# Attention and ResMLP in one kernel: the first batch's q and k loaded ahead of v with its exponentials in one chain, and lambda multiplied in PSUM in all blocks but the last

## The chip, the cores and the metric

One core of one Trainium2 chip. The time is the device time of one execution in microseconds (us). For one core there is no second die to compare with, so a run is called slow only when it lies over 1.5% above the fastest of the same kernel. The median of before is 381.8 us.

## The reference, cut to what matters

```python
# q, k, v: (8 batches, 8 heads, 576, 64); scores against k and v averaged over 8 rows
k_p = k.reshape(B, H, 72, 8, D).mean(axis=3);  v_p = v.reshape(B, H, 72, 8, D).mean(axis=3)
attn = softmax(q @ k_p.T / 8);  x = attn @ v_p            # x as (B, 576, 512)
a1 = alpha1 * x + beta1
u = x + lam * (w_tok @ a1)                                # token mix, over the 576 rows
ch = relu((alpha2 * u + beta2) @ w_ch1) @ w_ch2           # MLP 512 -> 2048 -> 512
out = u + lam * ch
```

The kernel cuts the 8 x 576 rows into 36 chunks of 128 and works on four chunks at a time: nine MLP blocks, numbered 0 to 8. While the MLP of block n runs on TensorE, the attention and token mix of batch n+1 are woven between its matmuls; so only batch 0 has nothing to hide behind. The 64 last rows of each head ("rest") are loaded and cast apart.

## The kernel before

The parts that the change and the argument touch. A number such as `at` is a place in the block's order of issue, counted in groups of TensorE work. Names in the views: `ps_...` lies in PSUM (`ps_sc` scores, `ps_h` and `ps_ch` the two matmuls of the MLP, `ps_tok` the token mix), `ET` are the exponentials, `x_tm` the normalised heads, `xs` these times lambda and alpha1, which the token mix takes in.

```python
    # loads of batch 0, in this order on the SyncE queue
    load_qk(0, 0); load_rem(0); load_v(0, 0); load_v_rem(0); load_qk(0, 1); load_v(0, 1)
    ...
    def sum_k(b, u, eng):                 # pool k: 16 -> 8 -> 4 rows, then a sum into bf16
        t = st1[b]["raw"][u][:, 1]
        for n in (4, 2):
            eng.tensor_tensor(out=t[:, :, 0:n], in0=t[:, :, 0:n], in1=t[:, :, n:2 * n], op=ALU.add)
        eng.tensor_tensor(out=bf, in0=..., in1=..., op=ALU.add)
    ...
    def scale_w2(g, i):                   # 16 of these, in block 1
        nc.vector.tensor_tensor(out=w2[g][:, i], in0=w2[g][:, i], in1=lam_bc, op=ALU.mult)
    ...
    def mlp_B(n, m, part):                # second matmul of the MLP; ps_ch has two PSUM buffers
        for j in js:
            nc.tensor.matmul(out=ps, lhsT=Hj[n, j][:, 128 * m:128 * m + 128],
                             rhs=w2[j // 4][:, j % 4, cols], start=(j == 0), stop=(j == NJ - 1))
        if part == 3 or last and part == 1:
            if n == 0:                    # block 0 runs before w2 is scaled
                nc.vector.tensor_tensor(out=ps, in0=lam_bc, in1=ps, op=ALU.mult)
            nc.vector.tensor_tensor(out=u, in0=u, in1=ps, op=ALU.add)
            nc.sync.dma_start(out=..., in_=u)
    ...
    # batch 1 (late = True) is woven into block 0
    todo = [(2.0 if late else -2.0, lambda: cast_rem(b, nc.gpsimd)), ...]     # rest q, rest k
    for u in range(2):                    # q_at = 0.5 and 6.0 for batch 1
        todo.append((q_at, lambda u=u, copy=copy: cast_q(b, u, copy)))
        todo.append((q_at + 0.1, lambda u=u: sum_k(b, u, nc.gpsimd)))
    ...
    if n == 1:
        for j in range(NJ):
            todo.append((0.5 + 1.1 * j, lambda j=j: scale_w2(j // 4, j % 4)))
```

The softmax here doesn't subtract the row's maximum and nothing guards it: scores larger than these inputs give would overflow.

## Time and profile before

| | before |
|---|---|
| device time, median of 4 runs | 381.81 us (381.28 to 382.54) |
| span of the profiled run, TensorE busy | 379.3 us, 361.6 us |
| first token mix starts, first MLP matmul starts | 27.28, 35.96 us |
| blocks 0 to 8, from first MLP matmul to first MLP matmul | 45.63, 43.46, 39.06, 38.86, 39.06, 38.87, 39.06, 27.62, 31.72 us |

A block is the time from its first MLP matmul to that of the next block, so the nine blocks and the 35.96 us ahead of them add up to the span. A block without waits is some 39 us when a batch is woven in and 27.6 us when none is (block 7).

### The profile page before, as it was taken

Reading aid. Unit: us, or ns where it says so; the run is one execution under the profiler, and the core shown is the slowest. Engines: PE = TensorE matmul, PEld = TensorE weight load, DVE = VectorE, ACT = ScalarE, POOL = GpSimd, SP = SyncE. Lnnn points to the kernel's source line nnn. Section 1 sums busy time; section 2 is a strip of 40 time slices with the busy share of each in tenths; the row PEclk is TensorE's granted clock in tenths of the full one; section 3 lists DMA queues with packets and bytes.
Section 4 is the critical chain, followed back from the end, with each engine's and each line's share of the span. In section 5 each row is a group of like instructions: output and inputs, shape, how many; then the busy total and the mean of one; then the engine's idle time right before and its main releaser. Section 6 shows DMA issues by size and latency. Waiting matters only on the chain.

```text
span 379.3 us, 6099 instructions
## 1 busy us (share of the span) xinstructions
PE 361.6 (95%) x2346; PEld 199.4 (53%) x2346; DVE 217.5 (57%) x441; ACT 202.6 (53%) x406; POOL 99.5 (26%) x141
## 2 busy tenths in 40 slices
PE   6579999999889999999999999999999999999995
PEld 2356754455444555455545554555455545544544
DVE  6976437799996528733864378436762685011011
ACT  3643887048721695179615970598049814721710
POOL 7743939003920082008200640055000000000000
PEclk9968999999999999999999999999999999999999
DMA  7999893029201561147013801290110011002002
GB/s 251 258 212 334 218 273 123 2 83 329 74 29 57 190 214 28 57 158 244 28 57 111 293 29 29 92 337 6 53 55 3 1 57 54 3 28 83 2 28 83
DMA packets 19602, 43.27 MB, mean 114 GB/s; under 512 B 2221, under 2 KB 4593, under 8 KB 19574
## 3 DMA queue, kind: packets, MB, share of 16 engines
q1 hardware_dynamic: 17488, 37.89, 29.4%
q0 software_dynamic: 1920, 4.86, 6.9%
q8 instruction: 18, 0.29, 0.3%
q10 hardware_dynamic: 166, 0.14, 0.1%
q14 instruction: 10, 0.08, 0.1%
HBM read 38.30 MB, written 9.44 MB: 126 GB/s over the span
## 4 chain that ended last, share of the span: by engine, by line
PE 82%; DVE 13%; ACT 1%; DMA 1%; issue 1%; SPq 0%
PE ps_ch L548 30%; PE ps_h L525 29%; PE ps_tok L494 12%; DVE w L319 3%; PE ps_sc L429 3%; DVE x_tm L453 2%; PE ps_uT L509 2%; PE ps_av L446 2%; DVE xs L460 1%; PE ps_q L346 1%; DMA qk_raw<-in_k_dram 1%; DVE qk_raw L132 1%; PE ps_kp L377 1%; DVE rec L451 1%; DVE v_u L392 1%
## 5 line engine op out<-in xcount | busy, mean ns | idle before, releaser
L548 PE MATMUL ps_ch<-w,Hj 128*128 128x512 bf16 (+1 forms) x592 | 140.2, 373 | 1.1 <-DVE w L319 1.1
L525 PE MATMUL ps_h<-u_fm,w 128*128 128x512 bf16 (+1 forms) x592 | 134.6, 373 | 0.2 <-ACT u_fm L511 0.2
L530 ACT ACTIVATE Hj<-ps_h,bias_cols 128x512 bf16<-128x512 f32 x144 | 96.7, 691 | 38.0 <-PE ps_h L525 37.1
L525 PEld LDWEIGHTS <-w 128*128 128x128 bf16 x592 | 64.8, 114 | 48.4 <-issue 0.9
L548 PEld LDWEIGHTS <-Hj 128*128 128x128 bf16 x592 | 55.7, 98 | 48.6 <-issue 0.5
L511 ACT COPY u_fm<-ps_uT 128x512 bf16<-128x512 bf16 x36 | 21.1, 586 | 89.1 <-PE ps_uT L509 89.0
L431 ACT ACTIVATE ET<-ps_sc 128x288 f16<-128x288 f32 (+1 forms) x128 | 52.4, 488 | 16.1 <-PE ps_sc L429 15.9
L555 DVE TENSOR_TENSOR u_sb<-u_sb,ps_ch 128x512 f32<-128x512 f32 (+1 forms) x37 | 24.8, 669 | 56.9 <-PE ps_ch L548 56.6
L494 PE MATMUL ps_tok<-xs,wtT 128*128 128x512 bf16 (+1 forms) x200 | 50.3, 385 | 2.0 <-DVE xs L460 1.9
L384 DVE CAST kpT<-ps_kp 64x288 bf16<-64x288 f32 x29 | 13.2, 455 | 49.2 <-PE ps_kp L380 49.0
L496 DVE TENSOR_TENSOR u_sb<-x_tm,ps_tok 128x512 f32<-128x512 f32 (+1 forms) x40 | 27.5, 686 | 22.5 <-PE ps_tok L494 22.5
L115 POOL CAST rem_q<-rem_raw 128x256 bf16<-128x256 f32 x7 | 3.1, 440 | 139.6 <-DMA rem_raw<-in_q_dram 139.6
L453 DVE TENSOR_TENSOR x_tm<-ps_av,rec 128x320 f32<-128x320 f32 x64 | 31.4, 491 | 2.3
L429 PE MATMUL ps_sc<-qT,kpT 128*128 128x288 bf16 (+1 forms) x128 | 29.2, 307 | 3.5 <-DVE x_tm L453 1.1
L494 PEld LDWEIGHTS <-wtT 128*128 128x128 bf16 (+1 forms) x200 | 19.3, 98 | 25.1 <-issue 3.6
L132 POOL TENSOR_TENSOR qk_raw<-qk_raw 128x512 f32<-128x512 f32 (+1 forms) x28 | 29.6, 1058 | 1.1
L498 DVE TENSOR_TENSOR u_bf<-u_sb,al_bc 128x512 bf16<-128x512 f32 (+1 forms) x39 | 27.8, 713 | 1.4
L446 PEld LDWEIGHTS <-ET 72*128 72x128 f16 (+1 forms) x256 | 16.8, 102 | 16.4 <-ACT ET L431 2.2
L451 DVE RECIPROCAL rec<-ps_av 128x5 f32<-128x5 f32 x64 | 12.0, 188 | 20.1 <-PE ps_av L449 19.6
L460 DVE TENSOR_TENSOR xs<-x_tm,lamal_bc 128x512 bf16<-128x512 f32 x30 | 21.9, 729 | 1.0
L446 PE MATMUL ps_av<-vp,ET 72*128 72x66 f16 (+1 forms) x256 | 19.0, 199 | 0.6 <-DVE x_tm L453 0.4
L392 DVE TENSOR_TENSOR v_u<-v_u 128x512 f32<-128x512 f32 (+1 forms) x30 | 17.6, 587 | 1.1 <-DMA v_u<-in_v_dram 0.4
(110 smaller groups left out, 290.8 us busy)
## 6 DMA issues: line engine op xcount, KB each, us to landing
qk_raw<-in_q_dram SPq DMA_DIRECT2D x16, 512.0 KB, 5.5
qk_raw<-in_k_dram SPq DMA_DIRECT2D x16, 512.0 KB, 6.3
v_u<-in_v_dram SPq DMA_DIRECT2D x32, 256.0 KB, 7.0
out_dram<-u_sb SPq DMA_DIRECT2D x32, 256.0 KB, 2.3
w<-in_moe_w_ch_dram POOLq DMA_DIRECT2D x2, 1024.0 KB, 12.8
w<-in_moe_w_ch_dram POOLq DMA_DIRECT2D x4, 512.0 KB, 9.8
rem_raw<-in_q_dram SPq DMA_DIRECT2D x8, 128.0 KB, 7.8
rem_raw<-in_k_dram SPq DMA_DIRECT2D x8, 128.0 KB, 5.3
```

Of the source, the lines that this page charges most:

```text
L132: eng.tensor_tensor(out=t[:, :, 0:n], in0=t[:, :, 0:n], in1=t[:, :, n:2 * n], op=ALU.add)
L429: nc.tensor.matmul(out=ps_sc[0:n, 0:288], lhsT=kpT_pool[u][:, j, r, 72 * hh:72 * hh + n], rhs=st["qT"][u][:, h % 4, :])
L431: nc.scalar.activation(out=ET[0:n, 64 + j:64 + S + j:2], in_=ps_sc[0:n, 0:288], func=AF.Exp, bias=0.0, scale=1.0 / 64)
L446: nc.tensor.matmul(out=av[:, c, :], lhsT=ET[:, m0:m0 + 256:2], rhs=vp1)
L453: nc.vector.tensor_tensor(out=x[:, :, dd:dd + D], in0=av[:, :, 0:64], in1=rec.unsqueeze(2).to_broadcast((P, 5, D)), op=ALU.mult)
L460: eng.tensor_tensor(out=xs[:, 0:4, cols], in0=x[:, 0:4, cols], in1=lamal_bc[:, cols].unsqueeze(1).to_broadcast((P, 4, D * (h1 - h0))), op= ...
L494: nc.tensor.matmul(out=ps_tok, lhsT=wtT[0:kk, at, t0:t0 + P], rhs=xs[0:kk, sc, :], start=(sc == 0), stop=(sc == 4))
L496: nc.vector.tensor_tensor(out=s["u"][p0:p1, :], in0=st1[b]["x"][p0:p1, c, :], in1=ps_tok[p0:p1, 0:DM], op=ALU.add)
L498: eng.tensor_tensor(out=s["u_bf"][p0:p1, :], in0=s["u"][p0:p1, :], in1=al2_bc[p0:p1, :], op=ALU.mult)
L525: nc.tensor.matmul(out=ps_h[:, t0:t1], lhsT=w1_of(cc, j), rhs=u_fm[n][:, cc, t0:t1], start=(cc == 0), stop=(cc == 3))
L530: nc.scalar.activation(out=t, in_=ps_h, func=AF.Relu, bias=bias_cols[:, j:j + 1], scale=1.0)
L548: nc.tensor.matmul(out=ps, lhsT=Hj[n, j][:, 128 * m:128 * m + 128], rhs=w2[j // 4][:, j % 4, cols], start=(j == 0), stop=(j == NJ - 1))
```

## The change

Two parts that touch each other nowhere. *Lambda*: `out = u + lam * ch` was had by scaling w2 once, 16 VectorE products in block 1. Now each block but the last multiplies its accumulator in PSUM, four products a block, and a scaled copy of w2 for block 8 is made in block 7, where VectorE is nearly idle. *First batch*: load the second half of q and k ahead of v, so that the exponentials of all eight heads can run on ScalarE in one chain; take casts, copies and products off VectorE; set up w_tok before the first token mix and not between the mixes. (In the part cut below, the two dummy matmuls ahead of the first mix, `keep_warm(2)`, also go.)

```diff
@@ loads @@
     load_qk(0, 0)
     load_rem(0)
+    load_qk(0, 1)
     load_v(0, 0)
     load_v_rem(0)
-    load_qk(0, 1)
     load_v(0, 1)
@@ constants @@
-    ET_pool = consts([P, S + 128], F16, "ET", 4)
+    ET_pool = consts([P, S + 128], F16, "ET", 6)
+    nc.vector.tensor_tensor(out=vecs[0:1, 1], in0=vecs[0:1, 1], in1=vecs[0:1, 0], op=ALU.mult)
@@ lambda @@
-    def scale_w2(g, i):
-        nc.vector.tensor_tensor(out=w2[g][:, i], in0=w2[g][:, i], in1=lam_bc, op=ALU.mult)
+    w2s = {}
+    def scale_w2(j):
+        if j % 8 == 0:
+            w2s[j // 8] = work.tile([P, 8, DM], BF, tag="qk_raw", bufs=2, name="w2_scaled")
+        nc.vector.tensor_tensor(
+            out=w2s[j // 8][:, j % 8], in0=w2[j // 4][:, j % 4], in1=lam_bc, op=ALU.mult)
+    def w2_of(n, j, cols):
+        return w2s[j // 8][:, j % 8, cols] if n == NBLK - 1 else w2[j // 4][:, j % 4, cols]
@@ mlp_B @@
-                             rhs=w2[j // 4][:, j % 4, cols], start=(j == 0), stop=(j == NJ - 1))
+                             rhs=w2_of(n, j, cols), start=(j == 0), stop=(j == NJ - 1))
-            if n == 0:
+            if n < NBLK - 1:
                 nc.vector.tensor_tensor(out=ps, in0=lam_bc, in1=ps, op=ALU.mult)
@@ first batch, cut @@
-    cast_rem(0, nc.gpsimd, nc.vector.tensor_copy)
+    cast_rem(0, nc.gpsimd)
+    cast_q(0, 1, nc.gpsimd.tensor_copy)
...
-    att_V(0, 0, nc.vector.tensor_copy)
     att_S(0, 2)
-    att_Vrem(0, nc.vector.tensor_copy)
     att_S(0, 3)
-    att_F(0, 1)
-    sum_k(0, 1, nc.vector)
+    sum_v(0, 0)
+    att_Vrem(0, nc.scalar.copy)
+    att_K(0, 1, nc.scalar.copy)
+    att_V(0, 0, nc.vector.tensor_copy)
     sum_v(0, 1, nc.gpsimd)
+    att_S(0, 4)
...
+    att_X(0, 4, 6, nc.gpsimd)
     load_w2(0)
     setup_wtok(0, nc.scalar.copy)
     att_AV(0, 6)
+    load_qk(1, 0, nc.vector)          # and the other loads of batch 1
+    ...
+    setup_wtok(1, nc.scalar.copy)
+    att_AV(0, 7)
+    att_X(0, 6, 8)
+    setup_rowsum(0); setup_wtok(2, nc.scalar.copy); setup_rowsum(1); setup_wtok(3, nc.scalar.copy)
     mix_T(0, 0)
-    setup_wtok(2, nc.scalar.copy)
-    setup_wtok(3, nc.scalar.copy)
@@ blocks @@
-        if n == 1:
+        if n == NBLK - 2:
             for j in range(NJ):
-                todo.append((0.5 + 1.1 * j, lambda j=j: scale_w2(j // 4, j % 4)))
+                todo.append((0.5 + 1.5 * j, lambda j=j: scale_w2(j)))
```

More of the change, by code (lines that the diff above doesn't have):

```diff
@@ L425, in att_S @@
         u, r, hh = h // 4, h // 2 % 2, h % 2
-        ET, n = ET_pool[h % 4], P if hh else SPG
+        ET, n = ET_pool[(8 * b + h) % 6], P if hh else SPG
         for j in range(2):
@@ L567 @@
     nc.scalar.copy(out=lam_bc, in_=ps_lam)
-    ps_al1 = broadcast(1)
+    ps_lamal = broadcast(1)
+    nc.scalar.copy(out=lamal_bc, in_=ps_lamal)
     cast_q(0, 0, nc.vector.tensor_copy)
@@ L572 @@
     sum_k(0, 0, nc.vector)
-    cast_rem(0, nc.gpsimd, nc.vector.tensor_copy)
+    cast_rem(0, nc.gpsimd)
+    cast_q(0, 1, nc.gpsimd.tensor_copy)
     keep_warm(2)
-    att_Frem(0, (0, 1), nc.scalar.copy)
-    att_K(0, 0, nc.scalar.copy)
-    sum_v(0, 0)
+    att_Frem(0, (0,), nc.scalar.copy)
+    att_K(0, 0, nc.vector.tensor_copy, nc.scalar.copy)
+    att_Frem(0, (1,), nc.vector.tensor_copy)
+    row_of_xs(0, nc.vector)
+    load_wtok()
     sum_v_rem(0, nc.gpsimd)
-    nc.vector.tensor_tensor(out=lamal_bc, in0=lam_bc, in1=ps_al1, op=ALU.mult)
-    cast_q(0, 1, nc.vector.tensor_copy)
-    load_wtok()
     for g in range(2):
@@ L585 @@
     att_S(0, 1)
-    att_V(0, 0, nc.vector.tensor_copy)
-    att_S(0, 2)
-    att_Vrem(0, nc.vector.tensor_copy)
-    att_S(0, 3)
-    att_F(0, 1)
-    sum_k(0, 1, nc.vector)
+    sum_k(0, 1, nc.vector)
+    att_F(0, 1)
+    att_S(0, 2)
+    att_S(0, 3)
+    sum_v(0, 0)
+    att_Vrem(0, nc.scalar.copy)
+    att_K(0, 1, nc.scalar.copy)
+    att_V(0, 0, nc.vector.tensor_copy)
     sum_v(0, 1, nc.gpsimd)
+    att_S(0, 4)
     att_AV(0, 0)
     att_AV(0, 1)
-    att_K(0, 1, nc.scalar.copy, nc.vector.tensor_copy)
-    att_S(0, 4)
+    att_S(0, 5)
     att_AV(0, 2)
-    att_S(0, 5)
+    att_X(0, 0, 2, nc.gpsimd)
     att_AV(0, 3)
-    att_X(0, 0, 2, nc.gpsimd)
+    att_X(0, 2, 4, nc.gpsimd)
     att_S(0, 6)
@@ L603 @@
     att_S(0, 7)
-    row_of_xs(0, nc.vector)
     att_AV(0, 4)
-    att_X(0, 2, 4, nc.gpsimd)
+    att_AV(0, 5)
+    att_X(0, 4, 6, nc.gpsimd)
     load_w2(0)
-    att_AV(0, 5)
     setup_wtok(0, nc.scalar.copy)
     att_AV(0, 6)
-    att_X(0, 4, 6)
-    att_AV(0, 7)
-    setup_wtok(1, nc.scalar.copy)
-    setup_rowsum(0)
-    setup_rowsum(1)
-    att_X(0, 6, 8)
     load_qk(1, 0, nc.vector)
@@ L622 @@
     load_v(1, 1)
-    keep_warm(2)
+    setup_wtok(1, nc.scalar.copy)
+    att_AV(0, 7)
+    att_X(0, 6, 8)
+    setup_rowsum(0)
+    setup_wtok(2, nc.scalar.copy)
+    setup_rowsum(1)
+    setup_wtok(3, nc.scalar.copy)
     mix_T(0, 0)
-    setup_wtok(2, nc.scalar.copy)
-    setup_wtok(3, nc.scalar.copy)
+    setup_rowsum(2)
+    mix_T(0, 1)
+    setup_rowsum(3)
     setup_vectors()
-    mix_T(0, 1)
-    setup_rowsum(2)
-    setup_rowsum(3)
     mix_T(0, 2, nc.gpsimd)
```

## The prediction

> **What bounds the kernel now.** I read the page's busy shares first (TensorE 361.6 us of 379.3, 95%, the next engine VectorE 57%), then cut the span into stages at the matmul groups, then followed the chain of waits inside the two stages that stand out. The table of stretches, with the columns span, busy time of each engine, granted TensorE clock, DMA share:
>
> ```profile
> core 0: us, PE busy (x) PEld busy (x) DVE busy (x) ACT busy (x) POOL busy (x), PEclk, DMA share, GB/s
> 0.00:35.96 35.96, 26.70 (x181) 15.37 (x182) 27.19 (x69) 17.07 (x38) 20.01 (x41) 0.86 0.97 257
> 35.96:81.59 45.63, 44.52 (x353) 26.30 (x352) 29.28 (x56) 27.03 (x57) 23.67 (x31) 1.00 0.53 151
> 81.59:125.01 43.42, 39.98 (x256) 21.40 (x255) 39.44 (x68) 22.80 (x46) 14.33 (x14) 1.00 0.34 119
> 125.01:164.07 39.06, 39.06 (x260) 21.66 (x259) 23.32 (x48) 22.97 (x47) 10.43 (x14) 1.00 0.36 119
> 320.00:347.70 27.70, 27.70 (x130) 13.60 (x129) 2.75 (x4) 11.00 (x16) 0.00 (x0) 1.00 0.10 38
> ```
>
> Rows one to four: the first batch's attention (no MLP matmul until 35.96), MLP block 0, block 1, block 2. Blocks 2 to 6 all take 38.9 to 39.1 us with TensorE never idle. Block 1 does the same matmuls and takes 43.42, with VectorE at 39.44 of it: 4.4 us more than block 2. The last row is block 7, where VectorE has 2.75 us of work in 27.70. So TensorE bounds everything except the first 36 us and block 1, and only those two can be shortened.
>
> The chain of waits in the first stage (start, length, what):
>
> ```profile
> 11.53 0.72 DVE q_bf L124
> ...
> 13.59 0.70 DVE qk_raw L132
> ...
> 14.31 1.75 DVE qk_raw L132
> ...
> 21.63 1.35 DVE xs L259
> ...
> 26.44 0.70 DVE xs L460
> ...
> 27.28 1.83 PE ps_tok L494 x5
> 29.12 1.07 PE ps_w L274 x10
> ```
>
> From 11 us to 27 us it is nearly all VectorE: the second half of q is cast there, then k is pooled there (its middle step takes 1.75 us, while the same step of the first half took 0.43), and a one-row product (xs L259, 1.35 us) stands in the middle of it. The first token mix begins at 27.28. From there to 35.96, 8.68 us, TensorE is always busy but the granted clock is 0.80, and ten transposes of w_tok (1.07 us) lie in between. In block 1 the chain names the scaling of w2:
>
> ```profile
> 84.46 2.49 DVE w L319 x4
> ...
> 98.25 4.09 DVE w L319 x3
> ```
>
> and the two kinds of product with lambda (columns after the count: min/median/max ns):
>
> ```profile
> L319 DVE TENSOR_TENSOR w<-w,lam_bc x16: 675/684/1755, 84.5 to 105.9; 128x512 bf16<-128x512 bf16 x16
> L554 DVE TENSOR_TENSOR ps_ch<-lam_bc,ps_ch x4: 685/690/697, 77.6 to 83.1; 128x512 f32<-128x512 f32 x4
> ```
>
> **What the Trainium skill says.** "Perfetto Trace Analysis", Optimization Strategy: a kernel can have several regimes with different most-contended engines, and one looks for the gaps inside each. The table above agrees. "SBUF — State Buffer", Who interferes with whom: a VectorE instruction with two SBUF inputs contends with a GpSimd instruction that reads SBUF, one with at most one SBUF input does not. The trace agrees: w2 scaling (two SBUF inputs) ranges from 0.675 to 1.755 us while GpSimd pools k, the product in PSUM (one SBUF input) stays within 0.685 to 0.697, though GpSimd was idle then, so that half isn't tested. "TensorE: Matmul & The Clock Gate", What's actually happening: after an idle window of about 3.4 us the clock halves. Here TensorE was busy 0.55 us in 15 to 18, and the granted clock in 18 to 24 was 0.50. "DMA: Bandwidth & Descriptors", Issuing engines are not separate DMA queues: all transfers interleave on the same engines. The DMA share of 0.97 over the first stage says that moving one load forward moves another back.
>
> **Part 1, lambda.** Removed from block 1: 16 scalings of w2, 13.7 us of VectorE (sum of the groups between 84.4 and 106.6). Put into block 7: the same 16, about 0.69 each = 11 us, beside 2.75 us of old work and 4 new products of 0.69 in 27.70 us, with GpSimd idle: hidden. The scaled copy takes the buffers of raw q and k, free by then. Added in blocks 1 to 7: four products in PSUM each, 4 x 0.69 = 2.8 us per block; block 0 has them already and block 8 stays without. Block 1 falls to a normal block: 43.42 - 39.06 = 4.4 us gained, a little less for the new products. In blocks 2 to 6 VectorE has 23 of 39 us, so 2.8 fit by sum, but not everywhere. The first accumulation of a block ends in the middle of the heads' normalisation, and from there VectorE works without a gap until the last xs columns, on which the token mix waits. In block 2 those end at 152.40 and the mix begins at 152.42: no slack, and 0.69 more goes straight to TensorE, less the 0.18 that TensorE itself would still be busy. In block 3 they end at 190.89 and TensorE gets there at about 191.6: 0.7 of slack, which just holds 0.69. So I take 0.5 us for blocks 2, 4 and 6 (whose batch is odd) and 0.15 for 1, 3 and 5: 2.0 in all. The later products fall between token mixes, where VectorE has 1.8 us of gaps in 10 us. **Net of part 1: -2.4 us.**
>
> **Part 2, the first batch.** The loads: 1.05 MB of q and k move ahead of 0.66 MB of v. By the bytes moved up to each time I put the second q at about 9.0 us and k at 10.5 (estimates; before they were used at 11.5 and 13.6). The cast of that q goes to GpSimd, also the cast of the rest rows; the rest of v goes from VectorE to ScalarE (2 x 0.42), the fourth copy of pooled k too (0.46), the third xs product to GpSimd (0.97). VectorE loses 0.54 + 0.67 (lam x alpha) + 0.80 + 0.84 + 0.46 + 0.97 = 4.3 us and the contention in k's pooling (1.3 us in the middle step). It gains one row product of 0.69 ahead of the first q cast, 0.3 us of fills for two more ET buffers, a k copy of 0.46 and a q copy of about 0.25: 1.7.
>
> Start: the row product waits for alpha (4.6 us) and delays the first cast by 0.35; the second broadcast matmul (2 us) waits for the row product and holds the q transposes from 6.6 to 7.4. ScalarE then copies lamal before q. So the first scores come at about 10.7 instead of 9.99, 0.7 us lost. Then ScalarE carries the chain: 16 exponentials at about 0.37 pitch (6.0), the q copy 1.0, v's rest 0.84, two k copies 0.8: 8.6 us plus about 1 us of waits, from 11.2 to about 20.8 (before: 22.2). VectorE's normalisation of eight heads (0.67 each) follows it and ends at about 23.8, and GpSimd's three xs products at 1.27 + 0.45 each, starting near 19.7, end at about 24.9; the last one on VectorE ends near 25. The first mix can begin at about 25.1: **-2.2 us**. Behind it the four mixes run with only small work between: 8.68 less 1.07 of w_tok transposes, less about half a microsecond if the clock is higher because TensorE idled less: 7.1. **-1.6 us**. Batch 1's loads are released at about 23 instead of 27.4, so block 0 is not held by them; w1's first half landed at 23.4 and might come 1 to 2 us later, still ahead of its first use near 31. Block 0 keeps its 45.6 us.
>
> Sum: -2.4 - 2.2 - 1.6 = -6.2. 381.9 - 6.2 = 375.7; I shade it to 375.2 for a clock that may not drop at all.
>
> **Rivals.** (a) The xs products on GpSimd, or the longer start, eat the new order: GpSimd's were 1.27 us against 0.69 on VectorE, and L464 took 0.91 once under contention. Then the first mix stays near 27 and only part 1 remains: 378.5 to 379.5. (b) The extra 28 products cost a full 0.69 or more in each of six blocks, because VectorE is in order and each of four delays can reach TensorE: 4 to 6 us lost, part 1 becomes nothing or negative, total 377.5 to 380. For it: block 2's zero slack. Against: only the first product of a block lies in a saturated run. (c) The clock never halves and VectorE's lighter load carries through (VectorE alone could finish xs near 22.4, counted from k's pooling at 11.6): first mix at 23, mixes in 6.5 us, 6.5 us gained at the start, total 372 to 373. (d) The DMA engines, full until 41 us, hold block 0 when it starts earlier. Against: the loads were finished by 41 and batch 1's last are needed near 44.
>
> **Range.** The threshold of 2% lies at 374.3, less than one microsecond below the estimate; the start could give 2 to 7, lambda 0 to 4. 80% range 371.5 to 378.5. A slowdown over 2% would need both parts to fail.
>
> **What would show it.** Right: block 1 at 39 to 39.5 us; block 2 about 0.5 longer, block 3 almost unchanged; block 7 at 27.7 still; first mix near 25, first MLP matmul near 32, with GpSimd's xs or the last VectorE xs ahead of it in the chain. Wrong: blocks 2 to 6 at 40 us, a gap ahead of block 8, exponentials that end after 22, or weights waited for at 31.

## More of the kernel before

The main views are in the prediction. One more is needed for what came after: what GpSimd does with batch 1 at the start of block 0. The columns are start, length, engine, line, operation, output and inputs, shapes, count, and in brackets an idle time ahead of it with what ended it.

```profile
35.68 1.03 POOL L124 CAST q_bf<-qk_raw 128x1024 bf16<-128x1024 f32 x1
36.68 2.52 POOL L132 TENSOR_TENSOR qk_raw<-qk_raw 128x512 f32<-128x512 f32 x2
...
39.95 0.40 POOL L115 CAST rem_q<-rem_raw 128x256 bf16<-128x256 f32 x1
```

Cast of q, pooling of k, cast of the rest rows of q follow each other without a gap: no bracket stands in these lines, so batch 1's transfers had landed.

## The result, and the profile after

The changed kernel takes 376.28 us (median of 4 runs, 375.66 to 376.92) against 381.81: the ratio is 0.985, with a 95% interval of 0.983 to 0.988. Within 2%, but clearly not equal. A ratio here is the mean time of one kernel's fast runs over that of the other's of the same rounds, so not quite the ratio of the medians quoted. In other rounds the gain was smaller: an unaltered second run of the changed kernel (below) gave 0.993 [0.989, 0.997].

Ledger of the two profiled spans (379.3 and 374.2 us):

| stage | before | after | difference | predicted |
|---|---|---|---|---|
| to the first token mix | 27.28 | 25.50 | -1.78 | -2.2 |
| first mix to first MLP matmul | 8.68 | 6.55 | -2.13 | -1.6 |
| block 0 | 45.63 | 46.90 | **+1.27** | 0 |
| block 1 | 43.46 | 39.11 | -4.35 | -4.4 and a little back |
| blocks 2, 4, 6 | 39.06, 39.06, 39.06 | 39.70, 39.64, 39.51 | +1.67 | +1.5 |
| blocks 3, 5 | 38.86, 38.87 | 38.92, 38.85 | +0.04 | +0.3 |
| block 7 | 27.62 | 27.62 | 0 | 0 |
| block 8 | 31.72 | 31.90 | +0.18 | 0 |
| sum | 379.3 | 374.2 | -5.1 | -6.2 |

The table of stretches of the kernel after, columns as in the prediction's (span, busy time of TensorE, its weight loads, VectorE, ScalarE, GpSimd, granted clock, DMA share, GB/s). The rows are the first stage, blocks 0, 1 and 2, and block 7:

```profile
0.00:32.05 32.05, 23.36 (x178) 13.42 (x180) 22.75 (x68) 18.45 (x40) 22.93 (x45) 0.95 0.96 243
32.05:78.95 46.90, 44.36 (x346) 26.30 (x351) 29.22 (x56) 27.23 (x57) 23.64 (x31) 1.00 0.59 177
78.95:118.06 39.11, 38.75 (x252) 21.33 (x255) 27.09 (x55) 22.37 (x46) 10.58 (x14) 1.00 0.39 132
118.06:157.76 39.70, 38.96 (x256) 21.65 (x259) 25.90 (x52) 22.95 (x47) 10.41 (x14) 1.00 0.36 117
314.60:342.20 27.60, 27.49 (x128) 13.58 (x128) 15.16 (x24) 11.00 (x16) 0.00 (x0) 1.00 0.10 39
```

VectorE has 22.75 us of work in the first stage (27.19 before), 27.09 in block 1 (39.44 before) and 15.16 in block 7 (2.75 before), and block 7 is no longer for it. The first stage's DMA share is 0.96 as before: it moved the same bytes in less time. Block 0 has the same work on every engine as before and is longer, so it must contain a wait. The chain of waits of the kernel after, of the first 40 us (start, length, what):

```profile
6.21 7.98 DMA rem_v_raw<-in_v_dram
...
23.42 0.49 DVE x_tm L464
...
25.84 9.24 DMA rem_raw<-in_k_dram
35.08 1.26 POOL qk_raw L132
...
37.95 0.35 POOL rem_q L115
38.30 0.05 issue
38.35 0.28 PE ps_qr L372 x2
```

Two long transfers stand in it. The first, the rest rows of v, pushed back by the q and k now loaded ahead of it, sets when values and heads can begin: it landed at about 14.2, ScalarE copied its product at 16.3 and the pooled k behind that, and the exponentials of heads 4 to 7 began at 17.93. So the last exponentials end at 22.10, hardly earlier than in before (22.18):

```profile
21.26 0.84 ACT L442 ACTIVATE ET<-ps_sc 128x288 f16<-128x288 f32 x2 [0.15 <-PE ps_sc L440]
```

```profile
20.67 1.51 ACT L431 ACTIVATE ET<-ps_sc 72x288 f16<-72x288 f32 x4
```

What comes earlier is what follows: VectorE's last normalisation ends at 24.55 (before 26.41). The second transfer is a new thing: batch 1's loads, issued at 24.0 instead of 27.4, land at about 35.0, and GpSimd and then TensorE wait for them. (The chain names the rest rows of k, which ended last on that queue; GpSimd's own instruction reads the main k.) GpSimd's timeline shows it, to be held against the lines of before:

```profile
31.76 1.03 POOL L124 CAST q_bf<-qk_raw 128x1024 bf16<-128x1024 f32 x1
35.06 2.09 POOL L132 TENSOR_TENSOR qk_raw<-qk_raw 128x512 f32<-128x512 f32 x2 [2.27 <-DMA rem_raw<-in_k_dram]
...
37.89 0.40 POOL L115 CAST rem_q<-rem_raw 128x256 bf16<-128x256 f32 x1
```

The cast of q comes 3.9 us earlier than before, the pooling of k 1.6, for between them is a wait of 2.27 us. The rest cast ends 5.84 + 0.40 us after the first MLP matmul (before 3.99 + 0.40), and the table of waits around it has this for TensorE (what waited, for what, us in total, times, longest):

```profile
PE ps_qr L372 <- POOL rem_q L115: 0.8, 1, 0.8
```

Lambda: the groups of the product in PSUM and of the w2 scaling (min/median/max ns, first and last start).

```profile
L565 DVE TENSOR_TENSOR ps_ch<-lam_bc,ps_ch x32: 678/696/697, 74.9 to 342.5; 128x512 f32<-128x512 f32 x32
L326 DVE TENSOR_TENSOR w_scaled<-w,lam_bc x16: 679/682/684, 316.2 to 336.9; 128x512 bf16<-128x512 bf16 x16
```

All 32 products take the same time. None of them ran beside a GpSimd instruction, though, in this trace or in any other, so they don't show what GpSimd would do to them. And block 2, before and after, where the token mix takes over from the last columns of xs:

```profile
152.11 0.29 DVE L464 TENSOR_TENSOR xs<-x_tm,lamal_bc 64x128 bf16<-64x128 f32 x1
152.42 0.38 PE L494 MATMUL ps_tok<-xs,wtT 128*128 128x512 bf16 x1
```

```profile
140.22 0.70 DVE L565 TENSOR_TENSOR ps_ch<-lam_bc,ps_ch 128x512 f32<-128x512 f32 x1
...
146.07 0.59 PE L505 MATMUL ps_tok<-xs,wtT 128*128 128x512 bf16 x2 [0.48 <-DVE xs L471]
```

Before, TensorE came to the mix just as xs was ready. After, a product of 0.70 us six microseconds earlier in the same run of VectorE work has become a wait of 0.48 us.

### The profile page after: what moved, and what is told of

It reads as the page before. It is cut to its first block, busy times and chain, and to the rows that moved or that the text cites. A ratio compares the mean times of both kernels' runs of the same rounds, so it can differ in the third digit from the quotient of the medians.

```text
span 374.2 us, 6081 instructions
## 1 busy us (share of the span) xinstructions
PE 355.8 (95%) x2301; PEld 197.2 (53%) x2344; DVE 226.9 (61%) x468; ACT 203.8 (54%) x408; POOL 98.8 (26%) x145
## 4 chain that ended last, share of the span: by engine, by line
PE 77%; DVE 12%; DMA 5%; SPq 2%; ACT 1%; issue 1%; POOL 1%; POOLq 0%
PE ps_h L536 32%; PE ps_ch L559 25%; PE ps_tok L505 11%; DVE x_tm L464 5%; DVE xs L471 3%; PE ps_sc L440 3%; DMA rem_raw<-in_k_dram 2%; DMA rem_v_raw<-in_v_dram 2%; PE ps_uT L520 2%; PE ps_q L357 2%; DVE rec L462 1%; DVE xs L475 1%; PE ps_av L457 1%; SPq L78 1%; PE ps_kp L388 1%
## 5 line engine op out<-in xcount | busy, mean ns | idle before, releaser
L536 PE MATMUL ps_h<-u_fm,w 128*128 128x512 bf16 (+1 forms) x574 | 133.2, 373 | 1.0 <-ACT u_fm L522 0.2
L559 PE MATMUL ps_ch<-w,Hj 128*128 128x512 bf16 x493 | 123.2, 379 | 0.9
L505 PE MATMUL ps_tok<-xs,wtT 128*128 128x512 bf16 (+1 forms) x196 | 48.5, 379 | 2.6 <-DVE xs L471 2.3
L566 DVE TENSOR_TENSOR u_sb<-u_sb,ps_ch 128x512 f32<-128x512 f32 (+1 forms) x37 | 24.9, 672 | 24.9 <-PE ps_ch L559 23.8
L565 DVE TENSOR_TENSOR ps_ch<-lam_bc,ps_ch 128x512 f32<-128x512 f32 x32 | 22.1, 691 | 19.8 <-PE ps_ch L559 19.5
L132 POOL TENSOR_TENSOR qk_raw<-qk_raw 128x512 f32<-128x512 f32 (+1 forms) x28 | 28.8, 1029 | 3.4 <-DMA rem_raw<-in_k_dram 2.3
```

The source lines that it names most:

```text
L505: nc.tensor.matmul(out=ps_tok, lhsT=wtT[0:kk, at, t0:t0 + P], rhs=xs[0:kk, sc, :], start=(sc == 0), stop=(sc == 4))
L536: nc.tensor.matmul(out=ps_h[:, t0:t1], lhsT=w1_of(cc, j), rhs=u_fm[n][:, cc, t0:t1], start=(cc == 0), stop=(cc == 3))
```

## The experiments

Twelve kernels, on two chips. The kernel before ran beside them each time, with medians of 380.38 (378.3 to 384.25, one slow run among seven), 379.88 (377.75 to 380.43) and 380.31 us (379.0 to 382.15). Its scatter of about 1% is as large as most effects sought, so the verdicts rest on the block times of the profiles, which repeat far better; the times are given beside them. All results are correct unless said.

### The two parts apart

`lam_alone`: the lambda hunks of the diff on the kernel before. `start_alone`: the changed kernel with those hunks undone.

> Lambda part alone on the kernel before. Theory: block 1 falls by 4.3 us to about 39.1, blocks 2, 4 and 6 grow by 0.4 to 0.65 us each, the rest unchanged: 381.8 - 4.3 + 1.7 = 379.2 us, ratio 0.993. Rival, that the products cost in every block and the gain of block 1 is lost: 381 to 382 us. Rival, that the parts depend on each other (block 1 gained only because the start changed): block 1 stays above 41 us.

> First batch's new order alone, w2 scaled in block 1 as before. Theory: first MLP matmul near 32.0 us (3.9 us earlier), block 0 about 1.4 us longer than before, block 1 again at 43.4 us: 381.8 - 2.5 = 379.3 us, ratio 0.9935. Rival, that block 0's extra 1.4 us come from the lambda part: block 0 at 45.6 us and 377.9 us.

Measured: `lam_alone` 379.71 us (377.97 to 381.18), ratio 0.999 [0.992, 1.006], which says little. Its blocks say more: 45.05, 39.23, 39.58, 39.04, 40.09, 39.03, 39.52, 27.63, 31.74. Block 1 is 4.2 shorter and blocks 2, 4 and 6 are longer, with the old start. `start_alone` took 377.1 us (376.13 to 378.68), ratio 0.993 [0.987, 0.999]; first mix 25.41, first MLP matmul 31.98, blocks 47.07, 43.47, then 38.86 to 39.07. The stretch of its block 1:

```profile
79.05:122.52 43.47, 39.76 (x251) 21.41 (x255) 39.45 (x68) 22.79 (x46) 14.42 (x14) 1.00 0.35 119
```

With w2 scaled there again VectorE is back at 39.45 us and the block at 43.47. So the parts are additive, block 1's gain is lambda's, and block 0's extra time belongs to the start.

`lam_alone` also has a second use: its start is the code of before. It ran the stretch from first mix to first MLP matmul at full clock. TensorE's busy time and granted clock from 27 to 30 and from 30 to 33 us, of before and of `lam_alone`:

```profile
27.00:30.00 3.00, 2.72 (x15) 0.63 1.08 227
30.00:33.00 3.00, 3.00 (x21) 0.80 0.99 366
```

```profile
27.00:30.00 3.00, 1.02 (x5) 1.00 1.00 172
30.00:33.00 3.00, 3.00 (x30) 1.00 0.97 321
```

That stretch took 8.68 us in before, 7.11 in `lam_alone` and 6.55 in after (also at 1.00). So of the 2.13 us gained there, 0.56 come with the new order at equal clock, and 1.57 are the clock of the profiled execution of before. This does not make the whole start look better than it is: `lam_alone` came to its first mix only at 28.98 and to its first MLP matmul at 36.09, no earlier than before at 35.96.

### The products

`no_product` drops them in blocks 1 to 7, which is wrong (relative error 1.67); `two_products` does them twice. Twice is wrong too, but lambda is so small that it passed the tolerance.

```diff
-            if n < NBLK - 1:          # no_product
+            if n == 0:
```

```diff
+            if 0 < n < NBLK - 1:      # two_products, behind the first
+                nc.vector.tensor_tensor(out=ps, in0=lam_bc, in1=ps, op=ALU.mult)
```

> The changed kernel without the products with lambda in blocks 1 to 7 (wrong result on purpose). Theory, that a product costs time only where the token mix has no slack: blocks 2, 4, 6 return to 39.0 us, blocks 1, 3, 5 stay at 38.9, together 1.7 us less than the changed kernel: 374.6 us. Rival, that the growth of blocks 2, 4, 6 has another cause (the two more ET buffers, other order): no change, 376.3 us.

> The changed kernel with the product made twice in blocks 1 to 7 (wrong result on purpose). Theory: the slack ahead of the token mix (0.7 us in blocks 3 and 5, none left now) is used up, so a second 0.69 us ahead of it goes to TensorE in each of blocks 1 to 6: blocks 2, 4, 6 at about 40.3 us, 1, 3, 5 at about 39.5; block 7 unchanged: 376.3 + 4 = 380.3 us. Rival, that VectorE still has room: under 1.5 us more.

Measured: `no_product` 373.43 us (373.28 to 373.65), blocks 1 to 6 38.86, 39.14, 38.87, 39.06, 38.86, 39.06. Against after the products cost 0.25, 0.56, 0.05, 0.58, 0 and 0.45: 1.9 us, where the prediction had 2.0. Its total lies 1.2 us under what I expected. Its block 0, 45.48, is 1.4 shorter than after's and its start 0.9 longer, a matter of the next experiments; the rest is not accounted for.

`two_products` took 387.32 us (386.88 to 387.42), 7 us more than expected: blocks 1 to 6 took 40.92, 41.52, 40.90, 41.70, 41.20 and 40.96, 1.45 to 2.35 more than after. The stretch of block 1, and the two waits of TensorE for VectorE in blocks 1 to 6:

```profile
78.91:119.83 40.92, 39.09 (x251) 21.23 (x255) 29.15 (x58) 22.37 (x46) 10.50 (x14) 1.00 0.37 126
```

```profile
PE ps_tok L505 <- DVE xs L471: 7.2, 6, 1.8
PE ps_uT L520 <- DVE u_bf L509: 3.2, 12, 0.4
```

VectorE is busy 29 of 41 us, and yet of 2.8 us more work most comes out at the end. The first 2.8 us per block cost 0.3 on average, the second 2.8 cost 1.45 to 2.35. So the share of busy time says nothing of the room left: VectorE's run from the middle of the heads to the mixes was nearly full, and the first product used up what was over.

### What lengthens block 0

Theory: batch 1's loads, released 3.4 us earlier into DMA engines that are full, land about as late as before; GpSimd, which takes its work in order, waits for k, and the rest rows of q behind it, which TensorE needs first, come late. Two ways to take the cause away: cast the rest of q on VectorE (`remq_dve`), or lighten the DMA engines by moving a load of w2 from there into block 0 (`w2_later`). `after_again` is the changed kernel unaltered, for the same rounds.

```diff
-        todo = [(2.0 if late else -2.0, lambda: cast_rem(b, nc.gpsimd)),
+        todo = [(2.0 if late else -2.0, lambda: cast_rem(b, nc.gpsimd, nc.vector.tensor_copy if late else None)),
```

```diff
-    load_w2(0)                                  # w2_later
-            for g in range(1, 4):
+            for g in range(4):
                 todo.append((3.0 + 1.5 * g, lambda g=g: load_w2(g)))
```

> The changed kernel once more, as the measure for the other runs on this chip. If block 0 ends when batch 1's data are there, and not a fixed time after its first matmul, then the first MLP matmul may move by 1 us between runs while block 0 still ends at 78.4 to 79.1 us. About 376.3 us.

> Changed kernel, the rest rows of q of batch 1 cast on VectorE, which is idle there, instead of on GpSimd behind k's pooling. Theory, that TensorE waits for GpSimd's queue: the wait of 0.8 us ahead of ps_qr is gone and block 0 ends about 1 us earlier, at 77.5 to 78: 375.3 us. Rival, that the rest rows' own transfer is late: the wait stays, with VectorE waiting for the transfer, and the time is that of the changed kernel.

> Changed kernel, the first quarter of w2 (needed only 22 us into block 0) loaded inside block 0 and not beside batch 1's q and k. Theory, that full DMA engines delay batch 1's k: GpSimd's wait of 2.3 us ahead of k's pooling is gone or under 1 us, block 0 ends near 78: 375.3 us. Rival, that the transfers ahead (w1) set the landing: no change. A loss would mean that w2 now arrives late: a wait ahead of ps_ch.

| | us | first MLP matmul | block 0 | TensorE's wait for rest q | GpSimd's wait for k |
|---|---|---|---|---|---|
| after | 376.28 | 32.05 | 46.90 | 0.8 | 2.3 |
| after_again | 376.76 (375.94 to 377.74) | 32.87 | 47.45 | 1.2 | 1.8 |
| remq_dve | 375.90 (374.96 to 376.58) | 32.62 | 45.80 | none | 1.8 |
| w2_later | 376.04 (374.68 to 376.77) | 32.69 | 46.28 | none | none |

The first row is from other rounds than the rest. GpSimd's pooling of batch 1's k in `w2_later`; its cast of q ends at 33.44, and no bracket stands here:

```profile
33.46 2.47 POOL L132 TENSOR_TENSOR qk_raw<-qk_raw 128x512 f32<-128x512 f32 x2
```

Both cures take TensorE's wait away, each at its own link. In `remq_dve` GpSimd still waits 1.8 us for k and is done pooling it at 38.1, but the rest of q was there by 35.5 us, VectorE cast it then, and TensorE came at 37.93 without a wait. In GpSimd's order it would have lain ready for 2.5 us behind something that was not. With less in flight, `w2_later` has k there some 1.8 us earlier relative to its use than `after_again`. The transfer of w2 is not the only one that counts: in `rest_v` (below), with w2 where it was, GpSimd didn't wait for k either; there the second half of w1 landed at 29.2, in after at 31.6. Other profiles of the same start agree: `start_alone` waited 1.2 us there and its block 0 took 47.07; `no_product` 0.3 us and 45.48; `two_products` had no wait and 45.71. (The profile puts the waits of the first two down to ScalarE, but the matmul starts at 38.67 and 38.65, and GpSimd's cast ends at 38.62 and 38.60.) Where TensorE waited for this cast for 0.8 us or more block 0 took 46.9 to 47.5; elsewhere, with the new start, 45.5 to 46.3. `rest_v` is the exception: 46.62 without this wait, because TensorE waited 1.2 us for two normalised heads instead. Since the wait ranges from 0 to 1.2 us with unaltered code, one profile without it proves little; that k came without any wait in `w2_later`, and that TensorE came at 37.93 in `remq_dve`, before GpSimd could have cast (38.1), is what carries the argument. Of the 1.27 us, 0.83 are this wait; after also waits 0.20 us for xs near the end of the block and 0.13 more than before for a head, which was not tested, and 0.1 is in no wait.

In time, the cures gain 0.9 and 0.7 us on `after_again` in the same rounds, with overlapping ranges: shown in the profile, not in the time. One reason is that the start gives and block 0 takes: blocks 0 of `no_product` and `two_products` started at 32.93 and 33.2, after's at 32.05, and all three ended between 78.4 and 79.0. But this is no rule: `after_again`, of which I had expected that its block 0 ends by 79.1, began it at 32.87 and ended it at 80.32.

### Is part of the gain only the clock?

`before_warm`: the kernel before, with nine matmuls on zeros put in the thin stretch of the first batch and eight instead of two ahead of the first mix, to keep the clock up.

```diff
+    keep_warm(9)
     att_K(0, 1, nc.scalar.copy, nc.vector.tensor_copy)
-    keep_warm(2)
+    keep_warm(8)
     mix_T(0, 0)
```

> Kernel before, with 7 and 6 more dummy matmuls in TensorE's two idle stretches of the first stage (about 14.5 to 17 and 25 to 27 us). Theory, that part of the gain of the changed kernel is that its clock is halved less often: granted clock over 0.995, first MLP matmul 1.5 to 2.5 us earlier than 35.96, about 379.3 us. Rival, that the first stage does not depend on TensorE's clock: 381.8 us (or what before takes on this chip) and no earlier MLP.

Measured: 378.95 us (378.12 to 380.95), ratio 0.998 [0.994, 1.002]. In the profiled run the clock from 24 to 27 us was 0.50 all the same, first mix 28.57, first MLP matmul 35.67. Inconclusive: the dummies did not keep the clock up. Only the scatter speaks. Of the 24 runs of before, those with a mean granted clock of 0.998 or more averaged 379.6 us (9 runs, one chip) and 379.3 (5, the other), those below it 381.2 (8) and 380.2 (2). So runs of before with the lower mean clock are 1 to 2 us longer, those of after, over its two labels, 0.6 (376.3 in five against 376.9 in three). The profiled run of before, at 0.987, was on the slow side. I hold it possible, not shown, that 1 to 2 us of the first comparison's 5.5 are this. Against it speaks the start: the three profiles with the old one (before, `lam_alone`, `before_warm`) come to the first MLP matmul at 35.96, 36.09 and 35.67, wherever their half-clock stretch lies, and the eight with the new one at 31.98 to 33.20, 3.3 us earlier on average.

### The load order by itself

`old_loads`: the changed kernel with v loaded ahead of the second q and k again. `rest_v`: only the rest of v ahead of v, its copies on VectorE and behind the second half of k, because the chain of after starts with this transfer.

```diff
     load_rem(0)                       # old_loads
-    load_qk(0, 1)
     load_v(0, 0)
     load_v_rem(0)
+    load_qk(0, 1)
```

```diff
+    load_v_rem(0)                     # rest_v
     load_v(0, 0)
-    load_v_rem(0)
...
-    att_Vrem(0, nc.scalar.copy)
     att_K(0, 1, nc.scalar.copy)
     att_V(0, 0, nc.vector.tensor_copy)
+    att_Vrem(0, nc.vector.tensor_copy)
```

> Changed kernel with the loads in the order of before (v ahead of the second half of q and k). If the load order itself is worth little, since the rest rows of v bound the chain in the changed kernel anyway: second q cast near 11.5 instead of 9.9, heads 4 to 7 within 0.5 us of 17.9, time within 0.7 us of the changed kernel (376.3 to 377). Rival, that loading q and k first is the heart of the change: first mix 1.5 us or more later, 377.5 us or more.

> Changed kernel, but the rest rows of v are loaded ahead of v's main part, and their product and copies (on VectorE) come behind pooled k's second half. Theory, that TensorE's 2 us wait for them holds the second half of the exponentials: heads 4 to 7 start near 16.7 instead of 17.9 us, the first mix begins near 24.3; but batch 1's data still set the end of block 0, so of this 1.2 us less than half reaches the end: 375.8 to 376.3 us. Rival, that the first stage alone sets the end: 375.1 us.

`old_loads` took 378.16 us (377.7 to 379.03), ratio 0.994 [0.991, 0.997]: 1.9 us more than after, though of other rounds, and 2.3 more than `rest_v` beside it. I had expected the load order to be worth little; that was wrong. Its first mix starts at 28.51, 3.0 later than after's. The pooling of k is where it goes:

```profile
13.45 1.84 DVE L132 TENSOR_TENSOR qk_raw<-qk_raw 128x512 f32<-128x512 f32 x2 [2.02 <-DMA qk_raw<-in_k_dram]
```

VectorE waits for that transfer for 2.02 us, and the sums then overlap with GpSimd's. But the 3.0 us are not all of this: in this profile, the slowest of the four runs, the granted clock was 0.50 from 15 to 27 us, in after only from 18 to 21. The times stand without it: the other three runs, at a clock of 0.999 or more, took 377.7 to 378.4 us, the three fastest of `rest_v` 374.8 to 375.9. Its block 0 is 45.49, without the wait: what the start loses there, block 0 gives half of back.

`rest_v` took 375.84 us (374.8 to 377.43), like after within the noise, but the mechanism I put forward did not happen: the first mix started at 26.57, not earlier. GpSimd, done with the rest 2 us earlier, pooled the second half of v while VectorE pooled the first:

```profile
13.81 3.35 DVE L403 TENSOR_TENSOR v_u<-v_u 128x512 f32<-128x512 f32 x2
15.59 2.15 POOL L403 TENSOR_TENSOR v_u<-v_u 128x512 f32<-128x512 f32 x2
```

The two sums took 3.35 us; in after, where GpSimd comes later, they took 1.15. TensorE then waited 3.53 us for the pooled v. The Trainium skill, "SBUF — State Buffer", section Who interferes with whom, says that a VectorE instruction with two SBUF inputs contends with a GpSimd one that reads SBUF. The trace agrees in part. Nearly all of the time is in VectorE's second sum, 14.65 to 17.16, 2.51 us where after has 0.42; GpSimd's first sum ran from 15.59 to 16.87. What held VectorE in the 0.94 us before that, while GpSimd was issuing loads of w1, is open.

### A later eviction, and all together

`late_evict`: in blocks 2, 4 and 6 the product and the sum of the first three accumulations are issued behind the xs columns, so that they no longer stand ahead of the mix. `best` joins it with `rest_v`, `w2_later` and `remq_dve`.

```diff
-        if part == 3 or last and part == 1:
+        if part == 3 and not late(n, m) or last and part == 1:
...
+            if late(n, m):            # n in (2, 4, 6) and m < 3
+                todo.append(((22.25, 25.85, 28.25)[m], lambda m=m: evict(n, m)))
```

> Changed kernel, the first three evictions (product and sum) of blocks 2, 4 and 6 moved on VectorE to behind the last xs product, behind two mixes and behind the last mix. Theory, that the 0.55 us of these blocks are the product standing ahead of xs: the wait for xs is gone, these blocks at 39.1 us instead of 39.6, 1.5 us less in all: 374.8 us. Rival, that VectorE's total in this stretch is the limit (as with two products): the wait moves to the transposes of u_bf and the blocks stay at 39.5.

> Changed kernel with rest_v, late_evict, w2_later and remq_dve together. If each holds: first mix near 24.3, block 0 not waiting (45.6 us from its first matmul), blocks 2, 4, 6 at 39.1: 376.3 - 1.2 - 1.3 - 1.5 = 372.3 us. If the first stage is bound by transfers whatever the order: 374 us.

A miss: 386.78 us (385.55 to 389.27), blocks 2, 4 and 6 at 43.76, 43.61 and 43.28. TensorE's wait, in the table of waits from 25 to 320 us:

```profile
PE ps_ch L559 <- DVE u_sb L574: 8.1, 3, 2.9
```

Three waits, one a block: the third accumulation takes the PSUM buffer of the first, which is free only when the first is evicted. With two buffers the eviction can't be put off that far. The blocks are 3.8 to 4.1 us longer than after's, the waits only 2.5 to 2.9: behind each of them the clock is at half speed for 3.4 us. TensorE's busy time and granted clock behind the wait that ends at 146.13:

```profile
146.00:149.00 3.00, 2.65 (x9) 0.74 0.39 89
149.00:152.00 3.00, 3.00 (x11) 0.69 0.01 4
```

`best` has the same fault: 386.72 us (382.8 to 387.94, 6 runs), with 43.41, 42.08 and 43.45 in those blocks. All three have the wait (2.5 to 2.9 us); block 4 alone has no half-clock stretch behind it, and is 1.35 us shorter. Its block 0, at 45.53, has no wait for the rest of q. So no version was shown to beat after. The joint version without `late_evict` was not run.

## Why the prediction was right or wrong

Predicted 375.2, measured 376.28, in the range and in the likeliest class. By its steps:

- **Block 1, -4.4: right.** -4.35, and `start_alone` and `lam_alone` both tie it to the w2 scaling.
- **The products, +2.0: right in size and in place.** 1.9 by `no_product`; 0.45 to 0.58 in blocks 2, 4, 6, next to nothing in 3 and 5, 0.25 in block 1. That they "fit by sum, but not everywhere" was the right reading; `two_products` shows that the next one would not have fitted anywhere. The scaling of w2 in block 7 is hidden, as said.
- **First mix at 25.1, -2.2: near in number, by another path, and so in part luck.** 25.5, -1.8 in the profiled pair; over the eight profiles with the new start (in `w2_later` without one load) 25.8 on average, over the two with the old start 28.1: -2.3. But the prediction gained its time on ScalarE, whose exponentials were to end at 20.8 instead of 22.2. They ended at 22.10; "exponentials that end after 22" was its own sign of being wrong, and it came true in six of these eight profiles. ScalarE had 9.1 us of work (predicted 8.6) and stood idle for 1.7 (predicted about 1), 0.9 of it for the rest rows of v, which the new load order had put back. The gain came on VectorE, behind the exponentials: with less other work there it ended the normalisation 2.45 us after them (predicted 3.0; 2.4 to 2.7 in the eight profiles, 4.2 to 4.3 with the old start), and the mix followed 0.95 us later (predicted 1.3). Exponentials 1.3 us late and 0.9 us less behind them made 0.4.
- **Mix to MLP, -1.6: the sum is right, its parts less so.** The prediction gave 1.07 to the transposes and half a microsecond to the clock. Measured 0.56 at equal clock and 1.57 from the clock in the profiled pair. Over the same eight and two profiles: 6.75 against 7.9, -1.15.
- **"Block 0 keeps its 45.6 us": wrong, and the largest part of the miss.** It took 46.9. Rival (d) named the mechanism, full DMA engines, and was set aside because "batch 1's last are needed near 44". The last transfer was not the one to look at. The first ones needed are: GpSimd wants k at 32.8, the landing was at about 35.0, and the rest of q, needed by TensorE at 37.5, stood behind it in GpSimd's order. The prediction had it at hand: it moved the loads and the first MLP matmul earlier by about the same time (3.4 and 3.9 us in the end), which is harmless only if the transfers take no longer, and it moved them into a stretch in which the DMA share was 1.1 (the view books a packet's whole time where it starts, so a share can pass 1).
- **The shade of 0.5 "for a clock that may not drop at all"** can't be held against anything: the clock was still 0.50 from 18 to 21 us in both profiles, and how often it falls into the mixes varies from run to run.

Had block 0 been given its 1.3, the sum would have been -4.9, near the 5.1 of the profiled spans.

## What to carry to other kernels

When a stage is made earlier, ask of every transfer that starts with it when its *first* user comes, not its last, and what stands behind that user in an engine that works in order: one late transfer there holds up work whose data have long come. What an added instruction costs is decided by whether it lies in the unbroken run ahead of what the bound engine waits for, and doubling it shows how much room was left, which the busy share does not. And before putting an eviction off, count the buffers that the accumulations rotate through.

## What the Trainium skill lacked or had wrong

- "SBUF — State Buffer", Who interferes with whom: that a VectorE instruction with at most one SBUF input doesn't contend with GpSimd, the half that the prediction left untested, agrees, though not by the products with lambda. The normalisation has one input in PSUM and one in SBUF; 26 of the 64 in after lay for more than half of their time under a GpSimd sum, cast or product, and all 64 took the same:

```profile
L464 DVE TENSOR_TENSOR x_tm<-ps_av,rec x64: 490/491/492, 19.0 to 301.7; 128x320 f32<-128x320 f32 x64
```

- What contention with two SBUF inputs costs, the same section gives by the order of issue: the later of the two instructions is held up. Here it was VectorE's in both cases looked at, though it had started first (GpSimd's spans are rough): 14.65 against GpSimd's 15.59 in `rest_v` (2.51 us instead of 0.42, GpSimd's 1.28), 14.31 against 14.46 in before (1.74 and 1.30).
- "TensorE: Matmul & The Clock Gate", Seeing it yourself: it warns that the clock's events in a trace can be unreliable. This agrees: in `remq_dve` the granted clock from 24 to 27 us reads 1.00, while the five matmuls of the first mix took 1.99 us and those of a later one 1.25. That trace has no clock event before 26.8 us, and the view prints 1.00 for want of one; in `lam_alone` the first is at 23.8, ahead of the stretch compared above.
- "DMA: Bandwidth & Descriptors": no figure for how long a transfer takes that shares full engines with others. Batch 1's k took about 10 us from issue (24.5) to landing (about 35) at a share of 1.1; the median of that kind in the run of before is 6.3.
- No page has what a put-off eviction costs with two PSUM buffers: here 2.5 to 2.9 us for each wait, and with the half-clock stretch behind it 3.8 to 4.1 us a block.
